# A decode attention block on one core: the code of TensorE and VectorE laid out with the loops first

## The chip, the cores and the metric

The kernel runs on one core of one Trainium2 chip. The metric is the device time of one execution in microseconds, the median of three runs. Five engines take part, each with its own stream of instructions: TensorE (PE in the profile, its weight loads PEld), VectorE (DVE), ScalarE (ACT), GpSimd (POOL) and SyncE (SP). Data come from HBM through 16 DMA engines. SP issues nearly all transfers, in program order, on one queue (q1 in the profile); ACT issues the small load of `x` on another (q10). Code reaches an engine by DMA too: the profile lists such packets under queues of the kind "instruction" (q8 and q14).

## The reference

One decode step for 8 sequences. `x` (8 x 512) is normalised; a grouped-query attention with 32 query heads and 8 key/value heads reads caches of 4096 positions; its result, through `wo`, is multiplied by a gate from a gated MLP on the same normalised input, and `x` is added.

```
xn = layernorm(x)
q = xn @ wq                                  # 8 x (32 heads x 128)
p = softmax(q . k_cache / sqrt(128))         # k_cache 8 x 8 x 4096 x 128, each head used by 4 queries
s = (p . v_cache) @ wo                       # v_cache as k_cache
z = gelu(xn @ w_in);  z1, z2 = halves(z)
g = silu((z1 * (w_sp * layernorm(z2) + b_sp)) @ w_out)
out = x + s * g
```

All is float32. Keys and values are 2 x 134 MB, the weights some 22 MB: about 290.7 MB are read for 32 KB of output.

## The kernel before

Three slots of 64 KB a partition (A, B, C; 8 MB each) take the big transfers in turn. First come `wq` (slot B, in two pieces), the MLP's weights (slot C) and the keys of the first half of head 0 (slot A). From then on a head (a round) takes four transfers of 8 MB: keys for sequences 0 to 3 into A, keys for 4 to 7 into B, values for 0 to 3 into C, values for 4 to 7 into B. A transfer is issued when TensorE has read what lay in its slot. After the last head `wo` comes into slot A in seven pieces of falling size (28, 16, 6, 6, 4, 2 and 2 KB a partition).

Ahead of the rounds TensorE and VectorE make the masks, the layernorm, all queries (L443 to L451) and the MLP's gate (L453 to L515). In a round TensorE forms the scores of all 8 sequences (L534), VectorE and ScalarE the softmax (L538 to L557), TensorE the products with the values (L566) and, after VectorE has reduced them (L568, L569), a small folding matmul for each sequence (L572). After the last round TensorE multiplies by `wo` (L593 for 28 of the 32 blocks, L601 for the rest), VectorE copies one partial sum in between (L637), and L647, L648 and the store L649 end the kernel.

The Python code records every operation, works out the semaphore waits, and then writes each engine's stream (`emit`). ScalarE, GpSimd and SyncE have all their rounds written out. TensorE and VectorE have a loop: TensorE of 8 rounds, VectorE of 7, with its last round written out behind the loop. In memory the stream of each of the two lies as it runs: the part ahead of the loop, the loop (L312 is the loop's register step and branch), the part behind it.

Of the kernel before, what the change touches and what calls it, by code (L numbers as in the profile page):

```python
# [43 lines left out]
class Region:  # L44


    def __init__(self, ap):
        self.name = ap.tensor.name
        row = 1
        for s in ap.tensor.shape[1:]:  # L50
            row *= s
        (_, np_), *free = ap.ap
        self.p0 = ap.offset // row
        self.p1 = self.p0 + np_
        at = np.array([ap.offset % row])
        for step, n in free:
            at = (at[:, None] + step * np.arange(n)[None, :]).reshape(-1)
        if str(ap.space) == "PSUM" or "PSUM" in str(ap.space):
            self.p0, self.p1 = 0, P
            banks = np.unique(at // BANK)  # L60
            at = (banks[:, None] * BANK + np.arange(BANK)[None, :]).reshape(-1)
        at = np.unique(at)
        self.lo, self.hi = int(at[0]), int(at[-1]) + 1
        self.at = None if len(at) == self.hi - self.lo else at
# [25 lines left out]
class Recorder:  # L90
# [5 lines left out]

    NAMES = ["tensor", "vector", "scalar", "gpsimd", "sync"]
    LOOPS = {"tensor": HKV, "vector": HKV - 1}

    def __init__(self, nc):  # L100
        self.nc = nc
# [16 lines left out]
    def add(self, eng, name, args, kw):  # L118
# [17 lines left out]
        if eng == "gpsimd" and name == "affine_select":  # L136
            op.reads += op.writes
        if self.now is not None and eng in self.LOOPS:
            op.iter, op.pos = self.now, self.count[eng]
# [33 lines left out]
    def plan(self):  # L173
# [22 lines left out]
        for (eng, pos), ops in groups.items():  # L196
            assert len({o.name for o in ops}) == 1, (eng, pos, {(o.name, o.line) for o in ops})
            need = set()
            for op in ops:
                for o in op.waits:  # L200
                    if o.dma:
                        assert eng == "tensor" or op.iter >= self.LOOPS[eng]
                    else:
# [16 lines left out]
        for ops in groups.values():  # L220
            for o in ops:
                if o.iter < self.LOOPS[o.eng]:
                    for q in ops:
                        if q.iter < self.LOOPS[o.eng]:
                            o.tokens = q.tokens = o.tokens | q.tokens
                            o.counted = q.counted = o.counted or q.counted

        for p in self.NAMES:
            for c in self.LOOPS:
                made = [o for o in self.order[p] if not o.dma and c in o.tokens]  # L230
# [23 lines left out]
    def emit_op(self, op):  # L254
        nc = self.nc
        eng = getattr(nc, op.eng)
        with nc.source_location(__file__, op.line, op.name):
# [27 lines left out]
            elif tells:  # L285
# [3 lines left out]
                    eng.wait_ge(own, 1).then_inc(t, 1)  # L289
                eng.wait_ge(own, 1).then_inc(own, -1)  # L290

    def emit(self):
        nc = self.nc
        for op in self.ops:
            op.round = None
        self.marks = {}
        for (h, ops) in self.heads.items():
            count = {}
            for op in ops:
                op.round, op.mark = h, op.pos if op.eng in self.LOOPS else count.get(op.eng, 0)  # L300
                count[op.eng] = count.get(op.eng, 0) + 1
                self.marks[h, op.eng, op.mark] = op
        self.plan()
        for n in ("scalar", "gpsimd", "sync"):
            for op in self.order[n]:
                self.emit_op(op)
        for n, rounds in self.LOOPS.items():
            ops = self.order[n]
            inside = [op for op in ops if op.iter is not None and op.iter < rounds]
            for op in ops[:inside[0].at]:  # L310
                self.emit_op(op)
            with getattr(nc, n).Fori(0, rounds):  # L312
                for op in inside:
                    if op.iter == 0:
                        self.emit_op(op)
            for op in ops[inside[-1].at + 1:]:
                self.emit_op(op)
        last = self.ops[-1]
        assert last.dma and last.eng == "sync"
        nc.sync.wait_ge(last.sem, 16)  # L320
        ids = [s.num for s in self.sems.values()]
        assert max(ids) - min(ids) + 1 == len(ids)
        nc.sync.sem_clear(range(min(ids), max(ids) + 1))
# [363 lines left out]
```

## Time and profile before

| | |
|---|---|
| median of 3 runs | 678.33 us (678.13 to 678.33) |
| profiled execution, its own time | 678.19 us |
| its span, first to last instruction | 676.9 us, 5989 instructions |
| busy share: PE, PEld, DVE, ACT, POOL | 55%, 17%, 24%, 2%, 1% |
| DMA | 290.85 MB, mean 430 GB/s over the span |
| mean granted TensorE clock | 0.766 |
| the chain that ended last | DMA of `wo` 6%, PE 2%, the rest below 1% |

The profiled execution took 1.3 us more than its span (678.19 less 676.9). The profile's DMA row is at 9 tenths in 39 of its 40 slices; in its GB/s row 35 of the slices stand at 434 or 435. Where a row of the timeline ends in brackets, they hold the time that the engine sat idle before it and what ended that wait.

### The profile page before, as it was taken

Reading aid. Unit: us, or ns where it says so; the run is one execution under the profiler, and the core shown is the slowest. Engines: PE = TensorE matmul, PEld = TensorE weight load, DVE = VectorE, ACT = ScalarE, POOL = GpSimd, SP = SyncE. Lnnn points to the kernel's source line nnn. Section 1 sums busy time; section 2 is a strip of 40 time slices with the busy share of each in tenths; the row PEclk is TensorE's granted clock in tenths of the full one; section 3 lists DMA queues with packets and bytes.
Section 4 is the critical chain, followed back from the end, with each engine's and each line's share of the span. In section 5 each row is a group of like instructions: output and inputs, shape, how many; then the busy total and the mean of one; then the engine's idle time right before and its main releaser. Section 6 shows DMA issues by size and latency. Waiting matters only on the chain. (4 is left out here: it accounts for less than half of the span.)

```text
span 676.9 us, 5989 instructions
## 1 busy us (share of the span) xinstructions
PE 375.3 (55%) x2570; PEld 117.4 (17%) x2570; DVE 165.1 (24%) x261; ACT 15.0 (2%) x35; POOL 4.3 (1%) x22
## 2 busy tenths in 40 slices
PE   2537554536665464555755355656745356655576
PEld 0112121102111121111211021111211021111221
DVE  2151033301430033401421024400422024400442
ACT  0000000000000000000000000000000000000000
POOL 1000000000000000000000000000000000000000
PEclk9987667888776567878767668876667788876679
DMA  9999999999999999999999999999999999999997
GB/s 388 434 435 435 434 434 434 435 434 434 434 434 434 434 434 434 434 434 434 434 434 434 434 434 434 434 434 434 434 434 434 434 434 434 438 434 434 449 413 314
DMA packets 6373, 290.85 MB, mean 430 GB/s; under 512 B 848, under 2 KB 864, under 8 KB 1504
## 3 DMA queue, kind: packets, MB, share of 16 engines
q1 hardware_dynamic: 6336, 290.75, 99.3%
q8 instruction: 4, 0.07, 0.0%
q10 hardware_dynamic: 32, 0.02, 0.0%
q14 instruction: 1, 0.01, 0.0%
HBM read 290.74 MB, written 0.03 MB: 430 GB/s over the span
## 5 line engine op out<-in xcount | busy, mean ns | idle before, releaser
L534 PE MATMUL sc<-slot_B,qz 128*32 128x512 f32 x512 | 74.4, 746 | 81.0 <-PEq L534 81.0
L566 PE MATMUL o_ps<-slot_B,tbuf 128*16 128x512 f32 x512 | 76.9, 728 | 63.9 <-PEq L566 63.9
L534 PE MATMUL sc<-slot_A,qz 128*32 128x512 f32 x512 | 72.1, 727 | 44.8 <-PEq L534 44.8
L566 PE MATMUL o_ps<-slot_C,tbuf 128*16 128x512 f32 x512 | 77.0, 742 | 14.6 <-PEq L566 14.6
L568 DVE TENSOR_TENSOR o_all<-o_ps,diag 128x512 f32<-128x512 f32 x64 | 44.2, 691 | 138.7 <-DVEq L568 138.7
L538 DVE TENSOR_REDUCE nm<-sc 128x1 f32<-128x1024 f32 x8 | 9.8, 1225 | 276.4 <-DVEq L538 276.4
L569 DVE TENSOR_REDUCE o_sb<-o_all 128x128 f32<-128x512 f32 x64 | 67.8, 1059 | 9.3
L534 PEld LDWEIGHTS sc<-slot_B,qz 128*32 128x32 f32 x512 | 20.4, 134 | 135.0 <-issue 135.0
L534 PEld LDWEIGHTS sc<-slot_A,qz 128*32 128x32 f32 x512 | 20.3, 131 | 90.2 <-issue 90.2
L572 PE MATMUL po<-fold,o_sb 128*128 128x4 f32 x128 | 24.4, 261 | 18.2 <-PEq L572 16.7
L572 PEld LDWEIGHTS po<-fold,o_sb 128*128 128x128 f32 x128 | 20.1, 197 | 74.3 <-issue 74.3
L566 PEld LDWEIGHTS o_ps<-slot_B,tbuf 128*16 128x16 f32 x512 | 13.4, 106 | 92.9 <-issue 92.4
L566 PEld LDWEIGHTS o_ps<-slot_C,tbuf 128*16 128x16 f32 x512 | 15.6, 112 | 56.8 <-issue 56.5
L556 PE MATMUL scr<-ident,pbuf 128*128 128x128 f32 x64 | 15.5, 424 | 13.4 <-PEq L556 13.4
L539 ACT ACTIVATE pbuf<-sc,nm 128x1024 f32<-128x1024 f32 x8 | 8.9, 1114 | 283.8 <-DVEq L538 283.8
L556 PEld LDWEIGHTS scr<-ident,pbuf 128*128 128x128 f32 x64 | 12.5, 223 | 13.8 <-issue 13.8
L443 PE MATMUL scr<-slot_B,xnT 128*32 128x512 f32 x64 | 10.7, 814 | 6.9 <-PEq L443 6.9
L557 DVE COPY tbuf<-scr 128x512 f32<-128x512 f32 x16 | 11.1, 692 | 12.3 <-DVEq L557 12.3
L542 PE MATMUL scr<-ident,nm 128*1 128x128 f32 x8 | 2.2, 269 | 13.7 <-PEq L542 13.7
L593 PE MATMUL sc<-slot_A,oT 128*8 128x512 f32 x56 | 7.6, 593 | 1.7 <-DMA slot_A<-in_wo 1.7
L549 PE MATMUL scr<-wl,same 128*128 128x1 f32 x16 | 3.6, 297 | 8.0 <-PEq L549 8.0
L623 ACT ACTIVATE oT<-po 128x32 f32<-128x32 f32 x7 | 1.4, 197 | 272.7 <-PE po L572 272.7
(100 smaller groups left out, 74.4 us busy)
## 6 DMA issues: line engine op xcount, KB each, us to landing
slot_B<-in_wq SPq DMA_DIRECT2D x1, 7168.0 KB, 21.2
slot_B<-in_v SPq DMA_DIRECT2D x1, 6144.0 KB, 25.8
slot_C<-in_w_mlp SPq DMA_DIRECT2D x1, 5376.0 KB, 33.4
slot_A<-in_wo SPq DMA_DIRECT2D x1, 3584.0 KB, 36.8
slot_B<-in_v SPq DMA_DIRECT2D x1, 2048.0 KB, 28.7
slot_A<-in_wo SPq DMA_DIRECT2D x1, 2048.0 KB, 41.2
slot_A<-in_wo SPq DMA_DIRECT2D x2, 768.0 KB, 43.3
slot_B<-in_wq SPq DMA_DIRECT2D x1, 1024.0 KB, 4.7
```

Of the source, the lines that this page charges most:

```text
L443: nc.tensor.matmul(pq[R * g:R * (g + 1), :], xnT[:, k, :], wq_sb[:, k, lo:lo + REP * DH], start=(k == 0), stop=(k == NK - 1))
L534: nc.tensor.matmul(sc[R * g:R * (g + 1), c, :], qz[:, b * R:(b + 1) * R], k_sb[:, i, c, g, :], start=(b == 0), stop=(b == B - 1))
L538: nc.vector.tensor_reduce(nm, sc, op=ALU.max, axis=AX.XY, negate=True)
L539: nc.scalar.activation(p.rearrange("p j s -> p (j s)"), sc.rearrange("p c s -> p (c s)"), AF.Exp, bias=nm, accum_out=l)
L549: nc.tensor.matmul(tot, same_all, wl, start=True, stop=True)
L556: nc.tensor.transpose(t[:, j * P:(j + 1) * P], p[:, 4 * c + j, :], ident)
L557: nc.vector.tensor_copy(pT[:, :, 4 * c:4 * c + 4].rearrange("p b j (g r) -> p (j g) b r", g=G), t.rearrange("p (m b r) -> p m b r", b=B, r ...
L566: nc.tensor.matmul(of[R * c:R * c + G * REP, :], pT[:, b, j, :], v_unit[:, j], start=(j < G), stop=(j >= J - G))
L568: nc.vector.tensor_mul(o_all[b % 2], o, diag[:, :, None].to_broadcast([P, G, DH]), after=after)
L569: nc.vector.tensor_reduce(o_sb[b % 2], o_all[b % 2].rearrange("p g d -> p d g"), op=ALU.add, axis=AX.X)
L572: nc.tensor.matmul(po[:, b * REP:(b + 1) * REP], o_sb[b % 2], fold, start=True, stop=True)
L593: nc.tensor.matmul(part[R * r:R * r + B, :], oT[:, h, r, :], wo_sb[:, m, :], start=(m < REP), stop=(m >= FOLDED - REP))
```

## The change

The code of TensorE and of VectorE is written in another order, and branches join the parts. The stream now begins with a branch to a part that holds nothing but another branch (`touch`) and lies behind the loop and behind the part ahead of the loop (`before`). From there the engine goes back to `before`, from its end to the loop (`rounds`), which lies first, and from the loop's end to `after`, which lies last, right behind `touch`. No operation, no wait and no transfer of the kernel is added, removed or changed; the other three engines' streams are as they were.

```diff
@@ class Recorder
     LOOPS = {"tensor": HKV, "vector": HKV - 1}
+    ROUNDS_AHEAD = ["tensor", "vector"]
@@
+    def emit_rounds(self, eng, rounds, inside):
+        with eng.Fori(0, rounds):
+            for op in inside:
+                if op.iter == 0:
+                    self.emit_op(op)
+
@@ def emit
             inside = [op for op in ops if op.iter is not None and op.iter < rounds]
-            for op in ops[:inside[0].at]:
-                self.emit_op(op)
-            with getattr(nc, n).Fori(0, rounds):
-                for op in inside:
-                    if op.iter == 0:
+            before, after = ops[:inside[0].at], ops[inside[-1].at + 1:]
+            eng, only = getattr(nc, n), [getattr(nc, n).engine]
+            ahead = n in self.ROUNDS_AHEAD
+            if ahead:
+                eng.br(f"{n}_touch")
+                with nc.body(f"{n}_rounds", valid_engines=only):
+                    self.emit_rounds(eng, rounds, inside)
+                    eng.br(f"{n}_after")
+                with nc.body(f"{n}_before", valid_engines=only):
+                    for op in before:
                         self.emit_op(op)
-            for op in ops[inside[-1].at + 1:]:
+                    eng.br(f"{n}_rounds")
+                with nc.body(f"{n}_touch", valid_engines=only):
+                    eng.nop(nofuse=True)
+                    eng.br(f"{n}_before")
+                nc.switch_bb(f"{n}_after")
+            else:
+                for op in before:
+                    self.emit_op(op)
+                self.emit_rounds(eng, rounds, inside)
+            for op in after:
                 self.emit_op(op)
```

TensorE's code before the change, from the end of the part ahead of the loop to the end of the code (the lines are those of the kernel before; `scr`, `sc`, `o_ps` and `po` are PSUM tiles, `qz` holds the queries):

```order
18 L502 MATMUL sc<-slot_C,tbuf 32x512 x7
19 L509 MATMUL scr<-tbuf,same 32x64 x8
20 L312 UNCONDITIONAL_BRANCH
21 L534 MATMUL sc<-slot_A,qz 32x512 x32
22 L534 MATMUL sc<-slot_B,qz 32x512 x32
```

The loop starts right behind the gate's last matmuls. The same engine's first rows in the changed kernel (all lines behind the new code are 21 higher, so L555 is the L534 of before):

```order
0 L321 UNCONDITIONAL_BRANCH
1 L294 UNCONDITIONAL_BRANCH
2 L555 MATMUL sc<-slot_A,qz 32x512 x32
3 L555 MATMUL sc<-slot_B,qz 32x512 x32
4 L563 MATMUL scr<-ident,nm 1x128
```

The first row is the branch to `touch`; the loop's code follows it. The end of TensorE's loop and what lies behind it in the changed kernel:

```order
21 L593 MATMUL po<-fold,o_sb 128x4 x2
22 L294 REGISTER_ALU
23 L294 COMPARE_AND_BRANCH
24 L324 UNCONDITIONAL_BRANCH
25 L443 MATMUL scr<-ident,tbuf 128x8 x4
26 L451 MATMUL scr<-pbuf,same 32x64 x8
```

The branch in row 24 leads from the loop to `after`; behind it lies the work with which the engine's run begins. The end of TensorE's code in the changed kernel:

```order
43 L523 MATMUL sc<-slot_C,tbuf 32x512 x7
44 L530 MATMUL scr<-tbuf,same 32x64 x8
45 L328 UNCONDITIONAL_BRANCH
46 L331 UNCONDITIONAL_BRANCH
47 L614 MATMUL sc<-slot_A,oT 8x512 x28
48 L622 MATMUL sc<-slot_A,oT_end 32x64 x8
```

Row 45 leads from `before` to the loop, row 46 is all of `touch`, and the multiplication by `wo` follows as the first of `after`. On VectorE the same five branches stand at the same places, and its `after` begins with its last round.

## Rows read from the trace of the kernel before

**Rows 1.** The page, DMA queues: packets, MB, share of 16 engines' span.

```profile
q1 hardware_dynamic: 6336, 290.75, 99.3%
q8 instruction: 4, 0.07, 0.0%
...
q14 instruction: 1, 0.01, 0.0%
```

**Rows 2.** Windows, the rounds: busy time per engine, then PEclk, DMA share, GB/s.

```profile
56.00:646.00 590.00, 331.76 (x2198) 103.96 (x2198) 140.48 (x202) 12.64 (x31) 1.47 (x7) 0.75 1.00 434
```

**Rows 3.** SP's timeline: start, us, issue of the slots' transfers.

```profile
1.64 0.42 SPq L367 DMA_DIRECT2D slot_C<-in_w_mlp  x1
2.11 0.65 SPq L575 DMA_DIRECT2D slot_A<-in_kT  x1
32.72 0.33 SPq L575 DMA_DIRECT2D slot_B<-in_kT  x1
54.02 0.33 SPq L580 DMA_DIRECT2D slot_C<-in_v  x1
```

**Rows 4.** DMA views around those issues: KB, us from issue to landing.

```profile
slot_C<-in_w_mlp SPq DMA_DIRECT2D x1, 5376.0 KB, 33.4
...
slot_A<-in_kT SPq DMA_DIRECT2D x1, 53.4
...
slot_B<-in_kT SPq DMA_DIRECT2D x1, 42.5
```

**Rows 5.** Timeline, 45 to 130 us: TensorE's first matmul on a landed slot.

```profile
75.36 8.59 PE L534 MATMUL sc<-slot_B,qz 128*32 128x512 f32 x64 [9.33 <-PEq L534]
...
94.67 5.72 PE L566 MATMUL o_ps<-slot_C,tbuf 128*16 128x512 f32 x32 [2.67 <-PEq L566]
...
113.96 3.62 PE L566 MATMUL o_ps<-slot_B,tbuf 128*16 128x512 f32 x16 [8.65 <-PEq L566]
```

**Rows 6.** DMA queues in windows 39:40.5, 66:67.2, 90:91, 126:127.2, 667:668, instruction packets alone.

```profile
q8 instruction: 1, 0.02, 4.0%
...
q8 instruction: 1, 0.02, 4.9%
...
q14 instruction: 1, 0.01, 1.9%
...
q8 instruction: 1, 0.02, 4.6%
...
q8 instruction: 1, 0.02, 5.5%
```

**Rows 7.** Timeline, the last 10 us.

```profile
668.07 2.93 PE L593 MATMUL sc<-slot_A,oT 128*8 128x512 f32 x22 [0.90 <-DMA slot_A<-in_wo]
...
671.81 1.04 PE L593 MATMUL sc<-slot_A,oT 128*8 128x512 f32 x6 [0.81 <-DMA slot_A<-in_wo]
672.91 0.69 DVE L637 COPY pbuf<-sc 128x512 f32<-128x512 f32 x1 [9.77 <-PE sc L593]
...
673.90 0.85 PE L601 MATMUL sc<-slot_A,oT_end 128*32 128x64 f32 x48
```

**Rows 8.** Timeline, the first 25 us.

```profile
0.73 0.90 ACTq L360 DMA_DIRECT2D pbuf<-in_x  x2
...
9.77 0.68 DVE L415 BATCH_NORM_STATS2 st<-pbuf 8x6 f32<-8x512 f32 x1 [6.13 <-DMA pbuf<-in_x]
...
22.50 5.12 PE L443 MATMUL scr<-slot_B,xnT 128*32 128x512 f32 x24 [6.87 <-PEq L443]
```

**Rows 9.** The loop's own line: duration ns min/median/max, first and last start.

```profile
L312 PEldq COMPARE_BRANCH  x8: 76/208/233, 127.5 to 663.4; - x8
...
L312 DVEq COMPARE_BRANCH  x7: 50/56/67, 126.3 to 588.6; - x7
```

**Rows 10.** Groups by line, two of the loop's: busy, mean ns | idle.

```profile
L534 PE MATMUL sc<-slot_A,qz 128*32 128x512 f32 x512 | 72.1, 727 | 44.8 <-PEq L534 44.8
...
L566 PEld LDWEIGHTS o_ps<-slot_C,tbuf 128*16 128x16 f32 x512 | 15.6, 112 | 56.8 <-issue 56.5
```

## The prediction

> **What bounds the kernel now.** I read the page's queues first. The data queue holds its 16 engines for 99.3% of the span [rows 1], and in the windows the rounds run at a DMA share of 1.00 and 434 GB/s [rows 2]. No engine is near that: TensorE is busy for 331.76 of 590 us there. The reader is to see that the kernel is one stream of 290.75 MB, and that the end moves only if the stream starts later, is starved, or is held up on the DMA engine that finishes last.
>
> Starved it is not. The keys for slot B are issued at 32.72 us, while the transfer ahead of them lands at 2.11 + 53.4 = 55.5; the first values are issued at 54.02, while those keys land at 32.72 + 42.5 = 75.2 [rows 3, 4]. So an issue stands some 21 us ahead of need at the start. Within a round TensorE idles 9.33, 2.67 and 8.65 us before it can begin on a slot, so it also has room there [rows 5].
>
> Held up it is, a little. A transfer of 8 MB on its turn takes 94.67 - 75.36 = 19.31 us, then 113.96 - 94.67 = 19.29 [rows 5]. But the first 8 MB of keys land 55.5 - (1.64 + 33.4) = 20.5 us after the MLP's weights, and the next 8 MB 75.2 - 55.5 = 19.7 us after those [rows 3, 4]. These two steps are 1.2 and 0.4 us too long, 1.6 together, with some 0.1 of rounding in it. What lies in them are two packets of code for TensorE, of 0.02 MB each: 4.0% of 16 engines over 1.5 us is 0.96 us of one engine, and 4.9% over 1.2 us is 0.94 [rows 6]. Two more come near 126 and 667 us (0.88 us each, by 4.6% of 1.2 us and 5.5% of 1 us), and one of 0.01 MB on the other instruction queue near 90 us (0.30 us). The steps that hold the packet of 90 us, and the one after, are back at 19.3. My reading: a packet of code delays the one DMA engine that carries it by about 1 us, for good, since that engine never gets free time to catch up; a transfer lands when the slowest of the 16 is through; the first two packets made an engine the slowest, and the others fell on engines that were ahead of it.
>
> The tail follows the landing. TensorE waits 0.81 us for a piece of `wo` before 671.81, then come six matmuls, VectorE's copy and the last matmuls [rows 7]. If the slowest engine ends earlier by some amount, all of that moves by it.
>
> **The change part by part.** *Branches.* Each of the two engines takes four new ones: to `touch`, to `before`, to the loop, to `after` (what stands at the loop's head was there). The nearest rows are the loop's own conditional branches, at a median of 0.21 us on TensorE and 0.06 on VectorE [rows 9], so 0.8 and 0.2 us in sum, of which three lie in the first 57 us. There an issue's lead of 21 us hides them, and for the one into the loop TensorE's 9.33 us of idling before slot B [rows 5]. The one to `after` delays TensorE's work on `wo`, which has two idle stretches of 0.90 and 0.81 us to give [rows 7]: 0.2 us of branch vanish in them. VectorE takes its last branch a round before the end. Cost: nothing. Without these covers it would be 0.8 us.
>
> *Where the packets of code go.* The same code has to arrive. Before, TensorE's code came block by block as the engine reached it, the last one while `wo` was being read [rows 6]. Now the first branch goes to the far end of the code, so code from there is wanted at about 0.7 us, at the moment when the first data are issued and the DMA engines have next to nothing to do; the block that holds `before` is wanted right after. Code for the loop lies at the head. I expect most of the five packets in the first 10 us.
>
> *What that is worth.* The gain is the 1.6 us of the two long steps, less what the early packets now cost on the engine that ends last. Bounds: at best nothing, if they go out ahead of the data (gain 1.6 us); at worst the 1.6 us again, if each delays its engine as before (gain 0). Below nothing is possible if two packets fall on one engine: another 0.96 us [rows 6], a loss of 1.0. I take a cost of 1.0 us, the engine time of one packet of TensorE's [rows 6] on one engine, since the block for `before` is asked for only once the branch in `touch` has run, with data already under way. Gain 0.6 us.
>
> *Stalls at the start.* TensorE and VectorE now wait for code before their first work. How long is not shown. From below it is the packet's own 0.94 us. From above I take the load of `x`, which the stream had begun to crowd: 9.77 - 0.73 = 9.0 us from its issue to its first reader [rows 8]. Two such waits in a row would be 18 us, and would push VectorE's first work past the arrival of `x`, and TensorE's queries past 22.50, where they wait for `wq` anyway, by 6.87 us [rows 8]; the lead of 21 us still covers the rest. Cost: nothing, at either end.
>
> The sum: 678.19 (the profiled run) - 0.6 = 677.6. The median stands 0.14 above the profiled run, so 677.7.
>
> [...] First the rows: one round of the loop holds at least 512 matmuls and weight loads (the two rows of [rows 10] are of eight such groups of 512 over 8 rounds), plus small ones; the loop's branch was taken back seven times, and the instruction queue of TensorE moved four packets in the whole run, none between 128 and 666 us [rows 1, 6]. So a branch back over a round did not fetch. [...]
>
> **The rivals.** *All early packets are free.* For it: the DMA engines are idle until the first data come, and none of the later steps shows a trace of code once it is in. Against it: three parts of the code are asked for one after the other, and only the first before the data. Time: 678.19 - 1.6 = 676.6, with the 0.14 some 676.7.
>
> *The packets only change place.* The blocks come in the stream after all, or cost the slowest engine the same 1.6 us at the start; or the code that `touch` brought is gone when it is needed, and is fetched again under cover. For it: the same number of bytes of code has to move, and an engine that is late stays late. Time: 678.3, or 679.3 with two packets on one engine.
>
> *Slower: TensorE stalls at the branch to `after`.* If the code brought by `touch` has been overwritten by the loop's 8 rounds, TensorE asks for it at 663.4 us, in a loaded stream, with nothing else to do. It has 0.90 + 0.81 = 1.7 us to give [rows 7]; a stall beyond that moves L593, the copy, the last matmuls and the store one for one. The stall lies between 0.94 and 9.0 us [rows 6, 8], so the loss between nothing and 7.3 us; at half of 9.0 it is 4.5 - 1.7 = 2.8, and the time 678.33 + 2.8 = 681.1. It decides from a stall of 1.7 us on. [...]
>
> **How the numbers follow.** Forecast (a part of the gain, 677.7): 0.48. All free (676.7): 0.15. Only moved (678.3 to 679.3): 0.25. Stall at the end (681.1): 0.12. What this kernel's measurement can tell from no change is about 0.2%, 1.36 us, so faster means below 676.97 and slower above 679.69. The first is most of the all-free case and a little of the forecast: 0.14. The second is the stall where it exceeds 3.1 us, and a little of the moved packets: 0.11. The same: 0.75. The range goes from the all-free case to a little above two packets on one engine: 676.7 to 679.5.
>
> **What would show it.** In the profile after: the instruction packets stand in the first 10 us, and none at 39, 66 or 126 us; the step from the MLP's weights to the first keys is 19.3 to 19.5 us and not 20.5; every slot of every round lands earlier by the same part of a microsecond; TensorE's idle before L614's second and third group is as it was. Wrong would be: instruction packets within the rounds; steps that are still long; a gap on TensorE at 663 us that no transfer ends; or a VectorE that starts so late that slot B is issued after 53 us. If the steps are all 19.3 and the end has not moved, my account of the slowest DMA engine is wrong.

## The result and the profile after

The changed kernel takes 679.53 us (median of 14 runs, 679.38 to 679.89), the kernel before, beside it, 678.23 us (678.12 to 678.75): a ratio of 1.002, 95% interval 1.0012 to 1.0027. That is 1.30 us slower, just outside the range, whose upper end was 679.5. The profiled run took 679.38 us with a span of 678.1, so its span is 1.2 us longer than before. Two executions stand apart from all others on record, one of the kernel before at 685.40 us, which the intervals below count, and one of the first experiment at 1102.27 us, which they do not.

The profile after, packets of code in windows 1:4, 8.5:11.5 and 668:670 (queue, count, MB, share of 16 engines over the window):

```profile
q8 instruction: 1, 0.02, 2.0%
q14 instruction: 1, 0.01, 1.1%
...
q8 instruction: 2, 0.03, 7.0%
...
q8 instruction: 1, 0.02, 2.7%
```

Three of TensorE's four packets and VectorE's one have moved into the first 12 us; one of TensorE's stays in the last 12. They answer to [rows 6]. The two near 9 us are in flight together, and they are dear: 7.0% of 16 engines over 3 us is 3.4 us of engine time for two, 1.7 us each, against 0.88 to 0.96 for each of TensorE's before.

The changed kernel's new branches (L321 to the far part, L331 from it, L324 from the loop to what follows; min/median/max in ns, first and last start):

```profile
L321 PEldq COMPARE_BRANCH  x1: 3452/3452/3452, 0.8 to 0.8; - x1
...
L331 PEldq COMPARE_BRANCH  x1: 8395/8395/8395, 4.3 to 4.3; - x1
...
L324 PEldq COMPARE_BRANCH  x1: 169/169/169, 664.8 to 664.8; - x1
...
L331 DVEq COMPARE_BRANCH  x1: 47/47/47, 1.3 to 1.3; - x1
```

TensorE waits 3.45 us for the far part and then 8.40 us for the part ahead of its loop, until 12.7 us. VectorE's branches to the far part and from it take 0.05 us each. The branch at 664.8 us takes 0.17 us, with no packet of code out between the pair near 9 us and the one at 668.8 us: the code behind the loop is there.

Where the time went shows in the landings. The changed kernel's page, issues (KB, us to landing), and the views around the first two loads of keys:

```profile
slot_B<-in_wq SPq DMA_DIRECT2D x1, 7168.0 KB, 23.8
...
slot_C<-in_w_mlp SPq DMA_DIRECT2D x1, 5376.0 KB, 36.0
...
slot_A<-in_kT SPq DMA_DIRECT2D x1, 54.9
...
slot_B<-in_kT SPq DMA_DIRECT2D x1, 41.6
```

The page of the kernel before had this for `wq`:

```profile
slot_B<-in_wq SPq DMA_DIRECT2D x1, 7168.0 KB, 21.2
```

The changed kernel's timeline: three issues, the arrival of `x`, TensorE's first matmul, the arrival of `wq`, the first matmuls on landed slots, and the tail:

```profile
1.64 0.42 SPq L388 DMA_DIRECT2D slot_C<-in_w_mlp  x1
2.11 1.17 SPq L596 DMA_DIRECT2D slot_A<-in_kT  x1
...
12.26 0.68 DVE L436 BATCH_NORM_STATS2 st<-pbuf 8x6 f32<-8x512 f32 x1 [8.54 <-DMA pbuf<-in_x]
...
14.57 0.59 PE L443 MATMUL scr<-ident,tbuf 8*128 8x8 f32 x4 [14.57 <-DVE tbuf L440]
...
25.14 4.42 PE L464 MATMUL scr<-slot_B,xnT 128*32 128x512 f32 x24 [7.03 <-PEq L464]
...
34.66 0.33 SPq L596 DMA_DIRECT2D slot_B<-in_kT  x1
...
76.42 8.67 PE L555 MATMUL sc<-slot_B,qz 128*32 128x512 f32 x64 [8.16 <-PEq L555]
...
95.73 5.80 PE L587 MATMUL o_ps<-slot_C,tbuf 128*16 128x512 f32 x32 [2.58 <-PEq L587]
...
115.04 3.61 PE L587 MATMUL o_ps<-slot_B,tbuf 128*16 128x512 f32 x16 [8.65 <-PEq L587]
...
669.24 2.93 PE L614 MATMUL sc<-slot_A,oT 128*8 128x512 f32 x22 [0.64 <-DMA slot_A<-in_wo]
...
672.98 1.04 PE L614 MATMUL sc<-slot_A,oT 128*8 128x512 f32 x6 [0.81 <-DMA slot_A<-in_wo]
```

Both `wq` and the MLP's weights land 2.6 us later than before (23.8 against 21.2; 36.0 against 33.4 [rows 4]), from the same issue times. The next two steps, too long before, are now 2.11 + 54.9 - (1.64 + 36.0) = 19.4 and 34.66 + 41.6 - 57.0 = 19.3 us. So 2.6 us are lost early and 1.5 of them come back where the packets of 39 and 66 us are gone; 1.1 remain. From there every slot starts by so much later: 76.42 against 75.36, 95.73 against 94.67, 115.04 against 113.96 [rows 5], and in the tail 672.98 against 671.81 [rows 7]. The stream was not starved: the second keys are issued at 34.66 us, 22 us ahead of the landing of the first at 57.0. TensorE's first matmul comes at 14.57 us and not at 12.09. It waits for VectorE and not for the branches, and VectorE waits for `x`, which it reads at 12.26 and not at 9.77 [rows 8].

### The profile page after: what moved, and what is told of

Same layout as the page of the kernel before. It is cut to its first block, busy times and chain, and to the rows that moved or that the text cites. A ratio compares the mean times of both kernels' runs of the same rounds, so it can differ in the third digit from the quotient of the medians.

```text
span 678.1 us, 5997 instructions
## 1 busy us (share of the span) xinstructions
PE 372.2 (55%) x2570; PEld 116.9 (17%) x2570; DVE 165.1 (24%) x261; ACT 15.0 (2%) x35; POOL 4.3 (1%) x22
## 3 DMA queue, kind: packets, MB, share of 16 engines
q1 hardware_dynamic: 6336, 290.75, 99.2%
## 5 line engine op out<-in xcount | busy, mean ns | idle before, releaser
L555 PE MATMUL sc<-slot_B,qz 128*32 128x512 f32 x512 | 73.2, 735 | 79.4 <-PEq L555 79.4
L555 PE MATMUL sc<-slot_A,qz 128*32 128x512 f32 x512 | 72.1, 727 | 44.8 <-PEq L555 44.8
L555 PEld LDWEIGHTS sc<-slot_B,qz 128*32 128x32 f32 x512 | 20.2, 132 | 132.4 <-issue 132.4
L555 PEld LDWEIGHTS sc<-slot_A,qz 128*32 128x32 f32 x512 | 19.9, 131 | 90.5 <-issue 90.5
## 6 DMA issues: line engine op xcount, KB each, us to landing
slot_B<-in_wq SPq DMA_DIRECT2D x1, 7168.0 KB, 23.8
```

Of the source, the lines that this page charges most:

```text
L555: nc.tensor.matmul(sc[R * g:R * (g + 1), c, :], qz[:, b * R:(b + 1) * R], k_sb[:, i, c, g, :], start=(b == 0), stop=(b == B - 1))
```

## The experiments

Three theories were set against each other. One: a packet of TensorE's code alone costs its DMA engine about 1 us, but two in flight together cost theirs some 2.5 us each. Two: any packet within the first 10 us of data is that dear. Three: TensorE's late start holds up the stream. All times are medians beside runs of the kernel before on the same chip, 678.23 to 678.33 us. The landing of `wq` in the kernel before is the 21.2 us above.

| kernel | TensorE's early packets | `wq`, us to landing | time, us | ratio, 95% interval |
|---|---|---|---|---|
| changed kernel | 1, then 2 together near 9 us | 23.8 | 679.53 | 1.0012 to 1.0027 |
| old order, far part kept | 1, then 1 near 9 us | 22.7 | 678.31 | 0.9991 to 1.0008 |
| loops first, no far part | 1, then 1 near 9 and 1 near 28 us | 22.6 | 678.41 | 0.9991 to 1.0009 |
| wait in the far part | 1, 1, 1 | 22.6 | 678.40 | 0.9992 to 1.0010 |
| wait ahead of the far part | 1, then 2 together near 22 us | 24.2 | 679.63 | 0.9993 to 1.0031 |
| VectorE's part alone | none | 22.1 | 678.24 | 0.9973 to 1.0012 |
| TensorE's part alone | 1, then 2 together near 9 us | 24.3 | 679.67 | 0.9993 to 1.0032 |

**The far part with the old order**, `before` ahead of `rounds` again, with the same branches:

```diff
                 eng.br(f"{n}_touch")
-                with nc.body(f"{n}_rounds", valid_engines=only):
-                    self.emit_rounds(eng, rounds, inside)
-                    eng.br(f"{n}_after")
                 with nc.body(f"{n}_before", valid_engines=only):
                     for op in before:
                         self.emit_op(op)
                     eng.br(f"{n}_rounds")
+                with nc.body(f"{n}_rounds", valid_engines=only):
+                    self.emit_rounds(eng, rounds, inside)
+                    eng.br(f"{n}_after")
                 with nc.body(f"{n}_touch", valid_engines=only):
```

> The branch to the far part stays, but the loop lies behind the part ahead of it again, so the second branch goes back to the head of the code, which is there at the start. Theory 1 (two packets of code for TensorE in flight together cost their two DMA engines some 2.5 us each, one alone about 1 us): the second branch asks for nothing, the packets come one at a time, 678.0 to 678.6 us. Theory 2 (a packet costs 2.5 us whenever it goes out within the first 10 us of data): one packet still goes out near 9 us, 679.3 to 679.7. Theory 3 (TensorE's late start holds up the stream): TensorE waits only once, its first matmul is near 12 us, 678.3.

Measured: 678.31 us. TensorE waits 3.34 us at its first branch and 0.18 at the second, and one packet goes out near 9 us (at 9.23). That is against theory two: a late packet of that moment does not cost 2.5 us. Theory three expected 678.3 here as well, so this kernel says nothing against it. What the far part brought did not last here: six packets of TensorE's came in all, four of them at 42, 68, 127 and 667 us, nearly the places of before.

**The loops first, without the far part:**

```diff
-                eng.br(f"{n}_touch")
+                eng.br(f"{n}_before")
...
-                with nc.body(f"{n}_touch", valid_engines=only):
-                    eng.nop(nofuse=True)
-                    eng.br(f"{n}_before")
```

> The loops lie first, and the first branch goes straight to the part ahead of the loop; there is no far part. One branch to code that is not there, and not two one after the other. Theory 1: the target's block comes near 2 us and the block behind it alone near 9 us, 678.0 to 678.6 us. Theory 2: the packet near 9 us still costs 2.5 us, 679.3 to 679.7. Theory 3: TensorE waits some 3.5 us instead of 12, its first matmul is near 12 us, 678.3.

Measured: 678.41 us, as theory one has it, and within 0.1 us as theory three has it. One wait of 3.83 us at the first branch, and a packet alone near 9 us. So the order with the loops first costs nothing by itself (678.41 beside 678.33 us), and by the kernel before this one neither does a branch to the far part and back to code that is there (678.31); together, as two branches in a row to code that is not there (waits of 3.45 and 8.40 us), they do: 679.53 beside 678.23.

**A wait in the far part** for the two halves of `x` (ScalarE's first two operations), so that one of the two packets near 9 us is in before the other is asked for:

```diff
                     eng.nop(nofuse=True)
+                    if n == "tensor":
+                        for op in self.order["scalar"][:2]:
+                            eng.wait_ge(op.sem, 16)
                     eng.br(f"{n}_before")
```

> The changed kernel, but TensorE waits in the far part until both halves of x have landed, before it branches to the part ahead of its loop. The same packets, the second pair no longer asked for together; TensorE starts later than in the changed kernel. Theory 1: the packets near 9 us come apart, each costs about 1 us, 678.0 to 678.6 us. Theory 2: the first of them still goes out near 9 us, 679.3 or more. Theory 3: TensorE starts still later (first matmul at 17 us or more), so slower than the changed kernel, 680 or more.

Measured: 678.40 us. This kernel's packets of code in windows 9:10.5 and 13:14.5:

```profile
q8 instruction: 1, 0.02, 3.9%
...
q8 instruction: 1, 0.02, 3.7%
```

The same code in the same order, 0.94 and 0.89 us of engine time each, and the loss is gone, though TensorE leaves the far part's branch only at 15.6 us and not at 12.7, and its first matmul comes at 15.67 and not at 14.57. Of the three theories only the first has this.

**The same wait ahead of the far part**, which moves the two packets together to a later time:

```diff
+                if n == "tensor":
+                    for op in self.order["scalar"][:2]:
+                        eng.wait_ge(op.sem, 16)
                 eng.br(f"{n}_touch")
```

> The changed kernel, but TensorE waits until both halves of x have landed before its first branch (the wait of the other experiment, put ahead of the far part and not into it). Theory 1: the two packets are asked for together again, now near 14 us, and cost some 2.5 us on their engines: 679.2 to 679.8 us. Theory 2 (it is the first 10 us that are dear): nothing goes out there but the first packet, 678.0 to 678.6. Theory 3 (TensorE's start): the latest start of all, 680 or more.

Measured: 679.63 us. This kernel's packets in windows 15:16.5 and 21.5:24:

```profile
q8 instruction: 1, 0.02, 4.0%
...
q8 instruction: 2, 0.03, 9.0%
```

One alone takes 0.96 us; the two together take 9.0% of 16 engines over 2.5 us, 3.6 us. The loss is back, at 22 us as at 9. TensorE's first matmul comes at 25.66 us, 11 us later than in the changed kernel, and the time is the same within 0.1 us: its start does not set the time, against theory three. The interval (0.9993 to 1.0031) holds 1, since one of the 27 runs of before took 685.4 us; the other 26 are at most 678.75 and all 11 of this kernel at least 679.55.

**One engine alone:**

```diff
-    ROUNDS_AHEAD = ["tensor", "vector"]
+    ROUNDS_AHEAD = ["vector"]
```

and in another kernel `["tensor"]`.

> Only VectorE's code is laid out anew; TensorE's is as before. One packet of 8 KB moves to some 3 us. Theory 1: no pair of TensorE's packets, 678.2 to 678.5 us, the packets at 39, 66 and 126 us as before. If VectorE's part of the change carried the loss, 679.5.

> Only TensorE's code is laid out anew; VectorE's is as before. Theory 1: the pair of packets near 9 us is there, 679.3 to 679.7 us. If the loss needs VectorE's packet too, 678.3.

Measured: 678.24 and 679.67 us (the second one's interval holds 1 for the same run of 685.4; all 11 of its runs are at least 679.49). The loss is TensorE's part. With VectorE's part alone, TensorE's packets came at 42, 68 and 107 us, where 39, 66 and 126 had been expected; `wq` landed 0.9 us later than before, with VectorE's packet out at 3.5 us, and the time did not change. The packets of the kernel with TensorE's part alone, in window 9:11.5:

```profile
q8 instruction: 2, 0.03, 9.1%
```

**Packet by packet.** The trace holds the start and the end of every DMA packet. In the running stream 16 packets of data are in flight, one for each engine, and the next one starts as one ends, so an engine's work can be followed. While the two packets of code run (changed kernel, TensorE's part alone, wait ahead of the far part), 14 packets of data are in flight: the two lie on two engines. In the changed kernel they take 1.36 and 2.01 us, and the packets of data right behind them 3.54 and 3.00 us where others of their size take 2.12; the two engines are 2.75 and 2.84 us late by then, in the other two kernels 3.0 to 3.1. A packet of TensorE's alone makes its engine 1.41 us late (at 39 and 66 us in the kernel before, near 9 us in the kernels with single packets): 0.88 to 0.97 of its own, the rest in the packet of data behind it. This is what the landings of `wq` show: 1.4 to 1.8 us later than before with single packets (23.0 us in the last experiment, the others in the table), 2.6 to 3.1 with a pair.

The delay stays with the engine: counted by bytes moved, the two engines of the changed kernel are 2.7 and 3.1 us behind the foremost at 20 us and 2.4 and 2.8 at 640 us, where the hindmost of the kernel before is 1.9 behind.

**The data held until TensorE's code is in:**

```diff
+        code = self.sem("code_in")
         for n in ("scalar", "gpsimd", "sync"):
+            if n == "sync":
+                nc.sync.wait_ge(code, 1)
...
                 with nc.body(f"{n}_before", valid_engines=only):
+                    if n == "tensor":
+                        eng.nop(nofuse=True).then_inc(code, 1)
                     for op in before:
```

> The changed kernel, but SyncE issues no data until TensorE has reached the part ahead of its loop, so that the code is in before the stream starts (x, which ScalarE issues, is not held). Whatever a packet costs in the stream is gone: both theories 1 and 2 expect all steps between the first landings at 19.3 us and a spread-free stream, with the end 1.2 us earlier relative to the first issue than in the kernel before; the time is that of before, less 1.2 us, plus the delay of the first issue (5 to 8 us): 682 to 685. Theory 3 expects the same relative to the first issue as the kernel before, 683 to 686; the long steps tell.

Measured: 686.88 us, above the expected 682 to 685, with the first data issue at 9.14 us. Its queues in windows 1.5:3 and 4.5:7.5, all that moved anything there, and the packet of code in 673.5:675:

```profile
q10 hardware_dynamic: 32, 0.02, 5.7%
q8 instruction: 1, 0.02, 4.3%
q14 instruction: 1, 0.01, 2.1%
...
q8 instruction: 2, 0.03, 7.8%
...
q8 instruction: 1, 0.02, 3.7%
```

With little but `x` in flight one packet takes 1.03 us, and with nothing else in flight two together take 3.74, 1.9 each. So what makes the packets of a pair long is the pair, and not the stream around them. But one expectation failed. The first two loads of keys are issued at 10.51 and 41.47 us:

```profile
slot_A<-in_kT SPq DMA_DIRECT2D x1, 52.4
...
slot_B<-in_kT SPq DMA_DIRECT2D x1, 40.8
```

Counted from the first issue they land 1.0 and 1.35 us earlier than in the kernel before, as foretold, and yet from the first issue to the last instruction this kernel takes 685.3 - 9.14 = 676.2 us, exactly as long as the kernel before (676.9 - 0.74). The gain was lost behind these landings; in the tail the packet near 674 us, of TensorE's code, still went out, which the next kernel tests.

**The same, and that packet fetched early as well:** a second far part lies behind the end of TensorE's code, and the first branch leads there.

```diff
-        for n, rounds in self.LOOPS.items():
+        for n, rounds in reversed(list(self.LOOPS.items())):
...
-                eng.br(f"{n}_touch")
+                eng.br(f"{n}_far" if n == "tensor" else f"{n}_touch")
...
-                nc.switch_bb(f"{n}_after")
+                if n == "tensor":
+                    with nc.body(f"{n}_after", valid_engines=only):
+                        for op in after:
+                            self.emit_op(op)
+                        eng.br(f"{n}_end")
+                    with nc.body(f"{n}_far", valid_engines=only):
+                        eng.nop(nofuse=True)
+                        eng.br(f"{n}_touch")
+                    nc.switch_bb(f"{n}_end")
+                    after = []
+                else:
+                    nc.switch_bb(f"{n}_after")
```

VectorE's code is written ahead of TensorE's here, so that the end of TensorE's comes last.

> The kernel whose data wait for TensorE's code, with one more far part behind the end of TensorE's code, to which the first branch leads. If the packet of code in the last 12 us is what took back the 1.2 us that the landings had won there, it is now gone from the end, and from the first data issue to the last instruction the time is 0.8 to 1.2 us shorter than in the kernel before: 676.1 to 675.1 us of span after the first issue, against 676.2. If the end holds another limit, the packet is gone and the 676.2 us stay. The whole time depends on how much later the first issue is (9 to 14 us).

Measured: 688.98 us, with the first data issue at 12.65 us. Its queues in window 660:688, no line of code among them, and its tail:

```profile
q1 hardware_dynamic: 1311, 10.52, 88.8%
...
683.05 1.04 PE L630 MATMUL sc<-slot_A,oT 128*8 128x512 f32 x6 [0.70 <-DMA slot_A<-in_wo]
...
685.14 0.85 PE L638 MATMUL sc<-slot_A,oT_end 128*32 128x64 f32 x48
```

From the first issue to the last instruction it now takes 688.1 - 12.65 = 675.45 us, 0.7 less than the kernel before. In these profiled runs, one of each kernel, that is what all packets of code in the stream cost the kernel before at its end; the spans of this kernel's five runs differ by as much (687.4 to 688.1), so the size is not sure. It is a little under the expected 0.8 to 1.2. To have them out of the stream in this way costs 11.9 us.

**An attempt at a faster kernel:** the far part behind the end of the code, left after a wait for `x`, and no hold on the data. The other lines are those of the kernel just shown.

```diff
...
+                    with nc.body(f"{n}_far", valid_engines=only):
+                        for op in self.order["scalar"][:2]:
+                            eng.wait_ge(op.sem, 16)
+                        eng.br(f"{n}_before")
```

> An attempt at a kernel faster than both: TensorE's first branch leads behind the end of its code, it waits there until x has landed, and then branches to the part ahead of its loop. Four packets of code for TensorE early, one at a time, and none in the last 12 us. Theory 1: each costs its engine about 1 us as any single packet does, so the slowest engine is 1.4 to 1.7 us behind as in the kernel before: 678.0 to 678.4 us, no gain clear of noise. If the packet in the last 12 us sets the end in the kernel before, 677.5 to 677.9. Theories 2 and 3: 679.3 or more.

Measured: 678.26 us beside 678.28 (interval 0.9991 to 1.0009). All four packets of TensorE's went out in the first 25 us one at a time, none later, and nothing was gained. So it is not the tail's packet in particular that sets the end: single packets in the stream, early or late, leave the end where it was, as long as they come one at a time.

## Why the prediction was wrong

*What bounds the kernel, and the lead of the issues:* right. Nothing in the changed kernel's rounds waits longer, and SP's issues stood 22 us ahead of need in spite of TensorE's start 2.5 us later, which came from `x`.

*Branches and stalls at the start cost nothing:* right as to the end. TensorE's stalls were 3.45 and 8.40 us, within the bounds of 0.94 and 9.0; VectorE, which had been expected to stall too, did not: its branches took 0.05 us each. Holding TensorE still longer (the wait in the far part) cost nothing either.

*Where the packets go:* right for four of five. The one of the tail stayed, which the list of what would show it did not foresee.

*The steps:* right. 19.4 and 19.3 us were foretold as 19.3 to 19.5.

*What that is worth:* this step failed, and with it the sign. It reads "I take a cost of 1.0 us, the engine time of one packet of TensorE's [rows 6] on one engine, since the block for `before` is asked for only once the branch in `touch` has run, with data already under way". Two things in it were wrong. The price was taken from the packet's own time, but a packet alone makes its engine 1.41 us late, and `wq` 1.4 to 1.5 in the three kernels of the table that send theirs one at a time. Against a return of 1.5 us that is no gain, and these kernels took 678.31 to 678.41 us. And the packet for `before` did not go out alone: two went out near 9 us, 0.3 us apart. One went out there in the old order as well (at 9.23 us), where the second branch took 0.18 us, and with a wait in the far part the two came apart, into windows 9:10.5 and 13:14.5. So it is likely that the branch to `before` called for only one of the two; what the other holds, and what called for it, no row shows. The two together cost 2.6 us at the landing of `wq`, not 1.0. Against a return of 1.5 us that is a loss of 1.1; the profiled span lost 1.2, the medians 1.30. The bound "below nothing", by "two packets fall on one engine", had nearly the size (679.3) by luck: the two fell on two engines, and each engine was late by twice what a single packet costs.

*The gain of 1.6 us at best* was too large as well. It was read from two long steps, as if all they held would come off the end. With every packet out of the stream the end came 0.7 us earlier, in one profiled run; with those of the first 130 us alone out, by nothing. In the stream the two kernels differ by the one packet in the tail, so it is likely that this kept the end in place.

*The stall at the branch to `after`* did not come: 0.17 us, for code brought in some 655 us earlier. So the third rival's condition, that the loop's rounds overwrite this code, did not hold here; how much code TensorE keeps was not shown. Stalls at branches there were, but at the start: 3.45 and 8.40 us, with packets of code on the way, against 0.18 for the second branch in the old order.

## What to carry to other kernels

This kernel runs at the rate of its DMA engines (the data queue held them for 99.2% of the changed kernel's span), and there code was traffic as well: a packet of it made one engine 1.4 us late, for 0.9 of its own, and with two engines 2.75 and 2.84 us late `wq` landed 2.6 us later. Moving such packets about gained nothing here while one of them remained in the stream (678.24 to 678.41 us beside 678.28 to 678.33), and two branches in a row to absent code put two in flight, which made `wq` 2.6 us later, against 1.4 for the same two apart. So look at the packets of code by window in the profile, and do not chain such branches; price a packet from the landings it delays, since its own duration says too little.

## What the runs showed that was not expected

Two packets of TensorE's code in flight together take 3.4 to 3.8 us of engine time in sum, in the stream or with no data in flight. One alone takes 0.88 to 0.97 in the running stream; the first ones, near 2 us, where small transfers are about, take 0.98 to 1.52. Why two slow each other, though they lie on two engines, was not tried and stays open. Why the packet of data right behind a packet of code is longer too, by some 0.5 us behind one alone and by 0.9 to 1.4 behind one of a pair, is open as well; with it, the 2.6 us of `wq` are accounted for.
